# A remade instruction order for a gated spectral/MLP mix: packed inverse rows, paired inverse tables, all weight splits remade on chip

## Chip, cores and metric

One core of one Trainium2 chip. The metric is the device time of one execution in microseconds (us), the median of several runs of each kernel.

## The reference, cut to what matters

```python
def reference(A_x, A_w_r, A_w_i, B_x, B_w1, B_b1, B_w2, B_b2, gate_w):
    x = A_x                                             # (1, 2048, 512), fp32
    g = sigmoid((x * gate_w).sum(-1, keepdims=True))
    a = irfft2(rfft2(x) * (w_r + 1j * w_i))             # over (2048, 512)
    b = gelu(x @ w1 + b1) @ w2 + b2                     # 512 -> 1792 -> 512
    return g * a + (1 - g) * b
```

## The kernel before, in words

**Products.** TensorE (PE) multiplies in the float32r format. A full fp32 operand is therefore kept as two tiles, a rounded high part `h` and the rest `l`, and a product is three matmuls (hh, hl, lh). Further matmuls are saved by a seven-product scheme (Strassen's) on pairs of the 14 blocks of 128 hidden columns (`seven`, L1093 on): its sums and differences of weights are made for the first half of the tokens (tiles `wA..`), stored in DRAM as `su` by L1085, and loaded again for the second half as `wB0h`, `wBth`, `wBsl` and so on (`raw`, issued through L411).

**Stages.** The 2048 rows are 16 tiles `j` of 128. `forward(j)` (L571) folds a tile and multiplies it by the tables of the column transform (`pd`) and of the row transform (`py`, tables `tf`), which gives `y`, one tile [128, 2, 257] per j. `stage1` (L745) is a radix-4 pass over the `y` tiles. Then come four passes of the MLP for the first half of the tokens, `group("A", p)` (L1138), with the filter `filt(q0)` (L749), which multiplies each `y` by a loaded tile `wf` (load L757; a small ACT operation on it L758, products `m` on DVE, L761). `stage4` (L783) is the last radix pass; the row 64 of its tiles is turned separately in `ownx`/`ownz` (load L796, store L802). `inverse(c, h)` (L804) handles two tiles at a time: it loads the tables `tg` (L810) and multiplies them by the gate `gb` (L811), loads the rows of `y` with halves exchanged into `sw` (L823, two loads of 63 rows for a tile; the two rows left are cleared by a memset on POOL, L819), forms `pq` (L825), multiplies (`pz`), splits the result into `zb` (L837 and L838), multiplies by `ci` (`pa`) and combines (`od`, `u`, `v`). `group("B", p)` is the MLP for the second half of the tokens, with the inverse transform of the other half running among it; `last` (L987) writes the output.

**Down projection.** `down` (L945) adds the blocks of a pass into a PSUM bank `po`. From the second pass on, the sum so far, `s`, is first copied into the bank by ACT (L966), and after the pass `po` is copied back to `s`. The weights are `wb0` to `wb13`, each as `h` and `l`. `load_w` (L886) makes them with `halve` (L878): one load of the raw weights into what will be `l` (L880), an ACT copy to `h` (rounding), an ACT copy of `-h` into `l` (L475), and a DMA on POOL's queue that adds the raw weights onto it from DRAM (L408, an accumulating DMA). The first half of the tokens (A) and the second (B) each need all 14 blocks. For blocks f below `KEPT` (10) the B passes make them again in this way; for f = 10 to 13, L904 stores `h` and `l` in DRAM (`sb..`) and the last B pass loads them (`wb10hb`, `wb10lb` and so on).

**What sets the order.** Every step is put into a graph (L228 to L345) with an engine, a cost and a lag. None of that is scheduled at run time: a long list, `ORDER`, gives the order in which steps are emitted, and each engine (PE, DVE, ACT, POOL and SP, which issues nearly all plain DMAs) works through its own steps in that order, waiting at each for what it needs. A second list, `SLOTS`, gives each tile its place among a few of its kind (7 of `t2k`, 3 tables `ttab`, 8 of `xhl`, 46 work tiles `w` of 256 KB, 8 PSUM banks); a tile's first writer waits for the last reader of the tile that had the place before. The costs in `dma`, `store` and `acc` (L400 to L408) belong to the search that made the lists and change nothing by themselves.

Of the kernel before, what the change touches and what calls it, by code (L numbers as in the profile page):

```python
# [10 lines left out]
F32 = mybir.dt.float32  # L11
F32R = mybir.dt.float32r
AF = mybir.ActivationFunctionType
ALU = mybir.AluOpType
# [12 lines left out]
KEPT = 10  # L27
# [28 lines left out]
def _tables():  # L56
# [39 lines left out]

    turn = np.pi * np.arange(NJ).reshape(4, 4) / NJ
# [251 lines left out]
def tile_kernel(ctx: ExitStack, tc: tile.TileContext, xt, xc, w1, w2, b1, b2, x0g, wf, wrev, out, consts):  # L349
# [50 lines left out]
    def dma(emit, kb, reads, writes, lag=3.4):  # L400
        return add("sp", 0.62 if kb == 257 else 0.47, lag, emit, reads, writes, kb / 340)

    def store(emit, kb, reads, writes):
        return dma(emit, kb, reads, writes, 3.8)
# [858 lines left out]
```

## Time and profile before

| | |
|---|---|
| median of 3 runs | 363.33 us (361.85 to 365.05) |
| the profiled execution | 362.7 us, its span 360.9 us |
| granted TensorE clock | 0.997 |
| DMA | 76.67 MB, mean 212 GB/s |
| plain DMA queue (q1) | 65.70 MB, 57.0% of 16 engines' span |
| software (accumulating) queue (q0) | 10.27 MB, 18.6% |

The profile's engines are PE (matmul), PEld (weight load, overlapping PE), DVE, ACT, POOL; SP issues DMAs, and SPq, DVEq and the like are the engines' queues, where issuing and waiting stand. A line "A Lx t <- B Ly: 3.1, 1, 3.1" in the table of waits says that engine A at line x, tile t, waited 3.1 us in all, once, longest 3.1 us, for what engine B did at line y (for a DMA, the transfer's names). The chain is followed back from the last instruction, through what released each; its rows are start, length, what. All matmuls go through one helper, so they have the line L414 and are told apart by tile. The idle time in 20 us stretches comes from the table of stretches, which gives for each the busy time of every engine.

### The profile page before, as it was taken

The numbers are of one execution on the slowest core, as the hardware profiler recorded it, in microseconds if no ns is written. First come the engines' busy times: TensorE is split into PE (matmuls) and PEld (weight loads), VectorE is DVE, ScalarE is ACT, GpSimd is POOL, SyncE is SP. The second block draws the span as 40 slices with busy tenths as digits, with TensorE's granted clock in tenths as the row PEclk, the third lists the DMA queues.
The fourth block names the chain that finished last, engine by engine and source line by source line (L and its number), as shares of the span: only waits on it lengthen the run. The fifth ranks groups of instructions, "written<-read, shape, count | busy, mean of one in ns | idle before, by whom it ended". The sixth has DMA issues, their size and how long they took to land.

```text
span 360.9 us, 5784 instructions
## 1 busy us (share of the span) xinstructions
PE 349.3 (97%) x1760; PEld 294.0 (81%) x1760; DVE 324.3 (90%) x681; ACT 266.7 (74%) x572; POOL 54.6 (15%) x84
## 2 busy tenths in 40 slices
PE   7999999999999999989999999999999999999994
PEld 6988888888887888868887888888888877788884
DVE  4999997989899999799999999999999787799951
ACT  4999999999999679767587993578866364577521
POOL 1012002001013002200010110002341330003320
PEclk9999999999999999999999999999999999999998
DMA  7999989249787947979996665696781678625697
GB/s 221 380 289 260 342 282 239 91 136 251 205 199 176 319 169 194 266 276 291 291 301 192 119 178 121 204 271 186 169 211 60 182 220 235 187 79 107 123 236 240
DMA packets 52041, 76.67 MB, mean 212 GB/s; under 512 B 5833, under 2 KB 23689, under 8 KB 52009
## 3 DMA queue, kind: packets, MB, share of 16 engines
q1 hardware_dynamic: 44728, 65.70, 57.0%
q0 software_dynamic: 6848, 10.27, 18.6%
q10 hardware_dynamic: 432, 0.33, 0.3%
q8 instruction: 14, 0.23, 0.3%
q14 instruction: 19, 0.15, 0.1%
HBM read 52.54 MB, written 19.41 MB: 199 GB/s over the span
## 4 chain that ended last, share of the span: by engine, by line
PE 82%; DMA 8%; SPq 5%; DVE 2%; issue 1%; ACT 1%; POOL 0%; DVEq 0%; POOLq 0%
PE po L414 39%; PE uxA L414 8%; PE uxB L414 8%; PE nuA L414 6%; PE nuB L414 6%; PE pd L414 4%; PE py L414 3%; PE ph L414 3%; SPq L823 2%; DMA wf<-in_wf 2%; PE pz L414 2%; DMA wBth<-su 2%; PE pa L414 2%; DMA g<-in_x0g 1%; DMA sw<-y 1%
## 5 line engine op out<-in xcount | busy, mean ns | idle before, releaser
L966 ACT ACTIVATE po<-s 128x512 f32<-128x512 f32 (+1 forms) x49 | 28.9, 595 | 10.1 <-DVE t L1004 4.7
L423 ACT ACTIVATE s<-po 128x512 f32<-128x512 f32 x40 | 23.5, 596 | 4.8 <-PE po L414 4.3
L761 DVE TENSOR_TENSOR m<-y,wf 128x514 f32<-128x514 f32 x32 | 21.4, 689 | 0.5
L819 POOL MEMSET sw<- 1x512 f32 x32 | 16.6, 518 | 27.9 <-PE po L414 15.2
L414 PE MATMUL py<-zb,tf 128*128 128x258 f32 x96 | 20.7, 297 | 0.0
L414 PE MATMUL pz<-tg,pq 128*128 128x128 f32 x128 | 18.9, 276 | 1.5 <-DVE tg L811 1.3
L414 PEld LDWEIGHTS pz<-tg,pq 128*128 128x128 f32 x128 | 17.4, 190 | 3.5 <-issue 1.8
L414 PE MATMUL pd<-cf,w 128*128 128x129 f32 x128 | 18.5, 275 | 0.3 <-DVE cf L533 0.3
L414 PEld LDWEIGHTS pd<-cf,w 128*128 128x128 f32 x128 | 17.2, 190 | 1.5 <-DVE cf L533 0.5
L976 ACT ACTIVATE s<-po,b2t 128x512 f32<-128x512 f32 x16 | 10.9, 690 | 9.6 <-PE po L414 9.6
L414 PE MATMUL pa<-zb,ci 128*128 128x256 f32 x96 | 17.3, 289 | 0.6 <-DVE zb L838 0.6
L414 PEld LDWEIGHTS py<-zb,tf 128*128 128x128 f32 x96 | 15.8, 189 | 2.1 <-ACT logit L617 0.2
L414 PEld LDWEIGHTS pa<-zb,ci 128*128 128x128 f32 x96 | 15.1, 189 | 2.9 <-DVE zb L838 1.0
L414 PE MATMUL nuB<-xB,wB0h 128*128 128x512 f32 x56 | 17.4, 391 | 0.0
L825 DVE TENSOR_TENSOR pq<-y,sw 128x256 f32<-128x256 f32 x32 | 12.8, 417 | 4.2 <-DMA sw<-y 3.3
L618 DVE TENSOR_TENSOR zb<-pd,zb 128x256 fp32r<-128x256 f32 x32 | 13.2, 419 | 3.6 <-ACT logit L617 3.5
L408 POOL DMA_DIRECT2D w<-bacc x8 | 9.6, 1255 | 41.3 <-ACT fiveB L423 26.7
L414 PE MATMUL nuA<-xA,wA0h 128*128 128x512 f32 x48 | 15.1, 396 | 0.0
L837 ACT ACTIVATE zb<-pz 128x512 fp32r<-128x512 f32 x16 | 9.0, 595 | 7.1 <-PE pa L414 4.8
L638 ACT ACTIVATE y<-pys 64x257 f32<-64x257 f32 x32 | 13.3, 417 | 0.9 <-DVE pys L635 0.3
L423 ACT ACTIVATE od<-pa 128x512 f32<-128x512 f32 x8 | 4.8, 598 | 11.9 <-PE pa L414 8.7
L408 POOL DMA_DIRECT2D wA0l<-in_w x6 | 5.4, 956 | 52.2 <-DMA tf<-tf 22.1
(541 smaller groups left out, 1240.8 us busy)
## 6 DMA issues: line engine op xcount, KB each, us to landing
wf<-in_wf SPq DMA_DIRECT2D x16, 257.0 KB
sw<-y SPq DMA_DIRECT2D x32, 126.0 KB
xf<-in_xt SPq DMA_DIRECT2D x14, 256.0 KB
tf<-tf SPq DMA_DIRECT2D x16, 192.0 KB
wrA<-in_w SPq DMA_DIRECT2D x12, 256.0 KB
xbA<-in_xc SPq DMA_DIRECT2D x8, 256.0 KB
xbB<-in_xc SPq DMA_DIRECT2D x8, 256.0 KB
bacc<-s SPq DMA_DIRECT2D x8, 256.0 KB
```

The costliest lines, as they stand in the source:

```text
L408: return add("pool", 0.9, 3.8, lambda: nc.gpsimd.dma_start(dst(), src(), accum_op=ALU.add), reads, writes, 2.3 * kb / 340)
L414: pe.matmul(ps, w, x, start=start, stop=stop, **more)
L423: a(lambda: act.activation(o.ap(), i.ap(), AF.Copy, scale=scale), n, [i], [o])
L618: v(lambda c=c: vec.tensor_tensor(segs(xl, c), both(c), segs(xh, c), op=ALU.subtract), 256, [ps[c], (xh, c)], [(xl, c)])
L638: a(lambda o=o, i=i: act.activation(Y[j].ap()[o:o + HP, 1], pys.ap()[i:i + HP, 1], AF.Copy), 257, [(pys, 1)], [(Y[j], 1 + k)], more=0.07)
L761: v(lambda mk=mk, k=k, y=y, w=w: vec.tensor_tensor(mk.ap(), y.ap(), w.ap()[:, k:k + 1, :ND].to_broadcast([P, 2, ND]), op=ALU.mult), 514, [ ...
L819: nc.gpsimd.memset(sw.ap()[o:o + 1], 0.0)
L823: dma(lambda sw=sw, y=y, o=o, i=i: sp.dma_start(sw.ap()[o + 1:o + HP], y.ap()[i + 1:i + HP, :, :HD]), 160, [y], [(sw, k)], 3.4)
L825: v(lambda sw=sw, pq_=pq_, y=y, k=k, op=op: vec.tensor_tensor(pq_.ap()[:, k], y.ap()[:, k, :HD], sw.ap()[:, 1 - k], op=op), 256, [y, TURNE ...
L837: a(lambda n=n, ps=ps: act.activation(zh.ap()[:, :, :, n], ps.ap(), AF.Copy), 512, [ps], [(zh, n)])
L966: a(lambda ps=ps, n=n, o=o: act.activation(ps.ap(), o.ap()[:, n], AF.Copy), size, [o], [ps], more=0.04)
L976: a(lambda o=o, ps=ps, q=q: act.activation(o.ap(), ps.ap(), AF.Identity, bias=b2t.ap()[:, q:q + 1]), 600, [b2t, ps], [o])
```

## The change

1. `ORDER` and `SLOTS` are made anew, 2105 steps for 2121, after the search's costs were set to other values (plain DMA lag 3.4 to 3.1 and rate 340 to 350, store lag 3.8 to 3.2, accumulating DMA lag 3.8 to 3.3).
2. `KEPT` goes from 10 to 14: no split is kept in DRAM. The eight stores of `sb10` to `sb13` and the eight loads in the last B pass go; in their place that pass makes four blocks by `halve`: four loads of raw weights, eight ACT operations, four accumulating DMAs. (The `if` of L904 and the `else` in `group` are still there, without use.)
3. The tables `tg` are laid out in pairs: each `inverse(c, h)` loads one tile of 128 KB and multiplies it once over 256 columns, in place of two loads of 64 KB and two multiplies of 128.
4. `stage4` writes its outputs packed (`YP`: the two halves of 256 follow each other, 2 KB of one piece a row, in place of two pieces of 1 KB in rows of 257), `ownx`, `ownz` and `sw` use them so. The `sw` loads move the same bytes.

Some steps and where they stand in the two lists (entry of 2121, entry of 2105):

| step | before | after |
|---|---|---|
| load of `wf6`, whose ACT step waits in the profile | 1026 | 1167 |
| load of `wBth3` | 1234 | 1152 |
| `tg`: first and last table load | 1395, 1990 | 1473, 1916 |

The diff without the two lists:

```diff
-KEPT = 10
+KEPT = 14
...
     ti[:, HP] = 1.0 - 2.0 * (np.arange(P) % 2)
+    ti = ti.reshape(2, 2, 4, P, P).transpose(2, 0, 3, 1, 4).reshape(4, 2, P, 2 * P)
...
-    def dma(emit, kb, reads, writes, lag=3.4):
-        return add("sp", 0.62 if kb == 257 else 0.47, lag, emit, reads, writes, kb / 340)
+    def dma(emit, kb, reads, writes, lag=3.1):
+        return add("sp", 0.62 if kb == 257 else 0.47, lag, emit, reads, writes, kb / 350)
     def store(emit, kb, reads, writes):
-        return dma(emit, kb, reads, writes, 3.8)
+        return dma(emit, kb, reads, writes, 3.2)
     def acc(dst, src, kb, reads, writes):
-        return add("pool", 0.9, 3.8, lambda: nc.gpsimd.dma_start(dst(), src(), accum_op=ALU.add), reads, writes, 2.3 * kb / 340)
+        return add("pool", 0.92, 3.3, lambda: nc.gpsimd.dma_start(dst(), src(), accum_op=ALU.add), reads, writes, 2.2 * kb / 350)
...
+    def packed(t):
+        return t.rearrange("p a b -> p (a b)")[:, :D].rearrange("p (a b) -> p a b", a=2)
+
+    YP = [View(yy, 3 * j, 3, lambda t, j=j: packed(t[:, j])) for j in range(NJ)]
...
     def stage4(j0):
         ys = [Y[j0 + 4 * q0] for q0 in range(4)]
-        radix4(ys, [j0 * q0 for q0 in range(4)], 1, HD, ys, f"d{j0}")
-        x, z = (t2k(f"own{n}{j0}", cls="own", parts=2) for n in "xz")
+        radix4(ys, [j0 * q0 for q0 in range(4)], 1, HD, [YP[j0 + 4 * q0] for q0 in range(4)], f"d{j0}")
+        x, z = (t2k(f"own{n}{j0}", HD, cls="own", parts=2) for n in "xz")
...
         def rows():
-            return yy.ap()[HP:HP + 1, j0::4].rearrange("p j a b -> p j (a b)")
+            return yy.ap()[HP:HP + 1, j0::4].rearrange("p j a b -> p j (a b)")[:, :, :D]
...
     def inverse(c, h):
+        tg = buf("ttab", [P, 2 * P], F32, f"tg{c}{h}", cls="tg")
+        dma(lambda: sp.dma_start(tg.ap(), ti_d[c, h]), 128, [], [tg])
+        v(lambda: vec.tensor_tensor(tg.ap(), tg.ap(), gb.ap()[:, c, 2 * h * P:(2 * h + 2) * P], op=ALU.mult), 2 * P, [gb], [tg])
         for n, j in enumerate((c + 8 * h, c + 8 * h + 4)):
-            t = buf("ttab", [P, P], F32, f"tg{j}", cls="tg")
-            dma(lambda t=t, j=j: sp.dma_start(t.ap(), ti_d[j]), 64, [], [t])
-            v(lambda t=t, j=j: vec.tensor_tensor(t.ap(), t.ap(), gb.ap()[:, j % 4, j // 4 * P:(j // 4 + 1) * P], op=ALU.mult), P,
-              [gb], [t])
-            y = Y[j]
+            y = YP[j]
...
-                dma(lambda sw=sw, y=y, o=o, i=i: sp.dma_start(sw.ap()[o + 1:o + HP], y.ap()[i + 1:i + HP, :, :HD]), 160, [y], [(sw, k)], 3.4)
+                dma(lambda sw=sw, y=y, o=o, i=i: sp.dma_start(sw.ap()[o + 1:o + HP], y.ap()[i + 1:i + HP]), 130, [y], [(sw, k)], 4.0)
...
-                    mm(ps.ap()[:, ft, k], pq_.ap()[:, k, ft * P:(ft + 1) * P], t.ap(), True, True)
+                    mm(ps.ap()[:, ft, k], pq_.ap()[:, k, ft * P:(ft + 1) * P], tg.ap()[:, n * P:(n + 1) * P], True, True)
```

More of the change, by code (lines that the diff above doesn't have):

```diff
@@ L793, in rows @@
         def rows():
-            return yy.ap()[HP:HP + 1, j0::4].rearrange("p j a b -> p j (a b)")
+            return yy.ap()[HP:HP + 1, j0::4].rearrange("p j a b -> p j (a b)")[:, :, :D]
         dma(lambda: sp.dma_start(flat(x.ap()[:4]), rows()), 8, ys, [x], 4.5)
-        a(lambda: act.activation(z.ap()[:4, :, :HD], x.ap()[:4, :, :HD], AF.Copy, scale=al.ap()[:, j0, 1:2]), 512, [x, al], [z], more=0.1)
+        a(lambda: act.activation(z.ap()[:4], x.ap()[:4], AF.Copy, scale=al.ap()[:, j0, 1:2]), 512, [x, al], [z], more=0.1)
         for k, op in enumerate((ALU.subtract, ALU.add)):
             v(lambda k=k, op=op: vec.scalar_tensor_tensor(
-                x.ap()[:4, k, :HD], x.ap()[:4, k, :HD], al.ap()[:, j0, 0:1], z.ap()[:4, 1 - k, :HD], op0=ALU.mult, op1=op), 256,
+                x.ap()[:4, k], x.ap()[:4, k], al.ap()[:, j0, 0:1], z.ap()[:4, 1 - k], op0=ALU.mult, op1=op), 256,
                 [z, al], [(x, k)], more=0.055)
@@ L822, in inverse, with turn @@
             for k, (o, i) in enumerate(((0, HP), (HP, 0))):
-                dma(lambda sw=sw, y=y, o=o, i=i: sp.dma_start(sw.ap()[o + 1:o + HP], y.ap()[i + 1:i + HP, :, :HD]), 160, [y], [(sw, k)], 3.4)
+                dma(lambda sw=sw, y=y, o=o, i=i: sp.dma_start(sw.ap()[o + 1:o + HP], y.ap()[i + 1:i + HP]), 130, [y], [(sw, k)], 4.0)
             for k, op in enumerate((ALU.subtract, ALU.add)):
                 v(lambda sw=sw, pq_=pq_, y=y, k=k, op=op: vec.tensor_tensor(
-                    pq_.ap()[:, k], y.ap()[:, k, :HD], sw.ap()[:, 1 - k], op=op), 256,
+                    pq_.ap()[:, k], y.ap()[:, k], sw.ap()[:, 1 - k], op=op), 256,
                     [y, TURNED[c], sw], [(pq_, k)])
             ps = bank([P, 2, 2, P], f"pz{j}", "pz")
-            def turn(k, t=t, ps=ps, pq_=pq_):
+            def turn(k, n=n, ps=ps, pq_=pq_):
                 for ft in range(2):
-                    mm(ps.ap()[:, ft, k], pq_.ap()[:, k, ft * P:(ft + 1) * P], t.ap(), True, True)
+                    mm(ps.ap()[:, ft, k], pq_.ap()[:, k, ft * P:(ft + 1) * P], tg.ap()[:, n * P:(n + 1) * P], True, True)
             for k in range(2):
-                add("pe", c_pe4(P, 2), 0.25, lambda k=k, turn=turn: turn(k), [t, (pq_, k)], [ps])
+                add("pe", c_pe4(P, 2), 0.25, lambda k=k, turn=turn: turn(k), [tg, (pq_, k)], [ps])
             a(lambda n=n, ps=ps: act.activation(zh.ap()[:, :, :, n], ps.ap(), AF.Copy), 512, [ps], [(zh, n)])
```

200 rows, old and new, of tables (ORDER, SLOTS) are left out of this document.

## The prediction

> **What bounds the kernel now.** I read the page first, for the engine that ends last.
>
> ```profile
> PE 349.3 (97%) x1760; PEld 294.0 (81%) x1760; DVE 324.3 (90%) x681; ACT 266.7 (74%) x572; POOL 54.6 (15%) x84
> ...
> PE 82%; DMA 8%; SPq 5%; DVE 2%; issue 1%; ACT 1%; POOL 0%; DVEq 0%; POOLq 0%
> ```
>
> TensorE (PE) is busy 349.3 of 360.9 us, and the change leaves its 1760 matmuls alone. So only its idle time can move: 11.6 us. The 18% of the chain that is not PE names what PE waits for: transfers (8%) and SP's issuing queue (5%). The table of stretches tells where the idle time is.
>
> ```profile
> 0.00:20.00 20.00, 17.84 (x109) 15.56 (x110) 15.41 (x48) 14.14 (x46) 2.29 (x13) 1.00 0.91 308
> 140.00:160.00 20.00, 18.39 (x80) 14.61 (x79) 16.92 (x34) 14.46 (x31) 2.60 (x3) 1.00 1.00 295
> 180.00:200.00 20.00, 19.16 (x85) 15.58 (x85) 19.83 (x39) 16.23 (x33) 3.52 (x5) 1.00 0.79 232
> 280.00:300.00 20.00, 19.21 (x113) 16.60 (x112) 16.33 (x38) 9.48 (x18) 7.24 (x14) 1.00 0.74 207
> 300.00:320.00 20.00, 18.64 (x105) 15.44 (x104) 15.54 (x38) 10.54 (x20) 0.00 (x0) 1.00 0.63 186
> 340.00:361.00 21.00, 16.04 (x85) 13.60 (x83) 9.29 (x17) 5.14 (x12) 4.42 (x4) 0.95 0.91 221
> ```
>
> After the length come busy PE, PEld, DVE, ACT and POOL, the granted clock, the DMA share and GB/s. The clock is 1.00, so nothing is throttled. PE's idle time is 2.16 at the start, 1.61, 0.84, 0.79 and 1.36 in the four middle stretches (4.60 together), 4.96 at the end; every other stretch is full. Next the waits, first of all engines and then PE's own, and the chain in order of time.
>
> ```profile
> DVE tg L811 <- DMA tg<-ti: 3.7, 3, 1.6
> DVE pq L825 <- DMA sw<-y: 3.3, 2, 2.2
> ACT wf L758 <- DMA wf<-in_wf: 3.1, 1, 3.1
> ```
>
> ```profile
> PE po L414 <- ACT po L966: 1.4, 1, 1.4
> PE pz L414 <- DVE tg L811: 1.3, 2, 0.8
> PE uxB L414 <- DMA wBth<-su: 0.8, 1, 0.8
> PE pa L414 <- DVE zb L838: 0.6, 1, 0.6
> ```
>
> ```profile
> 127.48 1.36 PE uxA L414 x6
> ...
> 147.09 8.77 DMA wf<-in_wf
> ...
> 184.13 6.75 DMA wBth<-su
> 191.03 1.61 PE uxB L414 x6
> ...
> 289.57 3.73 DMA tg<-ti
> ...
> 305.45 4.02 DMA sw<-y
> ...
> 343.57 12.48 PE po L414 x66
> ```
>
> Three separate stories. (A) At 147.09 a `wf` load is issued while the DMA engines are full (share 1.00); it lands 8.77 us later. ACT stands 3.1 us at L758, and the bias copy `po` (L966) behind it on ACT makes PE wait. (B) At 184.13 the load of `wBth` lands 6.75 us later, 0.8 us too late. (C) From 282 to 315 PE waits for the inverse's tables `tg` and swapped rows `sw`.
>
> "Busy" ends are modelled, so a pause is partly booked as work. I therefore also set each matmul's start against the work ahead of it at the undisturbed pace (1.36 for six of 512 columns, the first line above). By that account A costs 2.1, B 1.0 and C 4.0 us: 7.1 in the middle, against the floor of 4.6 from the table. I use 7.1, and the floor for the range. A slow drift of 1.5 us between 20 and 105 us stays as it is.
>
> **Change, part by part. The order.** I walked both lists and gave each step its place in TensorE work. For A, the raw load of `wb10l` moves up from 128 to 101 us of work and its ACT pieces from 143 to 128, so less is issued beside the `wf` load; every `wf` load now has over 9.5 us from the release of its slot to its use, above the 8.77 it took in a full stretch. For B, the load has 17.7 us ahead of its user instead of 6.1, against 6.75 measured; the shortest such loop up to 190 is 8.8. I take both as gone: 2.1 + 1.0 = 3.1, bounds 2.4 (1.61 + 0.84) and 3.1. If that cover fails again, each costs what it costs now.
>
> **Fewer splits in DRAM.** Eight stores of 256 KB leave the time around A and B, eight loads become four, and four accumulating loads on POOL and eight ACT operations are added, all for the last pass.
>
> ```profile
> L475 ACT ACTIVATE wb13l<-wb13h x1: 616/616/616, 143.3 to 143.3; 128x512 fp32r<-128x512 f32 x1
> L408 POOL DMA_DIRECT2D wb13l<-in_w x1: 1320/1320/1320, 145.0 to 145.0; - x1
> ...
> DMA to landing us min/median/max: 9.4/9.4/9.4
> ```
>
> Those 2 MB are 7 us of DMA time at the 295 GB/s of the full stretch; that supports taking them as gone, and isn't counted twice. ACT gets 8 x 0.62 = 5.0 us more between about 260 and 330, where it is busy 9.48 and 10.54 of 20: hidden, 0 (5.0 if all of it stood ahead of a bias copy). Four accumulations at 0.85 to 1.32 are 3.4 to 5.3 us of POOL, idle from 300 to 320: 0. They landed after up to 9.4 us when queued together; the new order leaves 11.4 us between `wb10l`'s ACT copy and its first matmul. So 0, with 2.0 us to spare; each further us of lateness of ACT there would cost a us.
>
> **Tables in one transfer.**
>
> ```profile
> L811 DVE TENSOR_TENSOR tg<-tg,gb x16: 274/285/293, 249.1 to 329.5; 128x128 f32<-128x128 f32 x16
> ```
>
> ```profile
> L810 SPq DMA_DIRECT2D tg<-ti x16: 318/373/1483, 221.4 to 323.5; - x16
> ```
>
> ```profile
> L825 DVE TENSOR_TENSOR pq<-y,sw 128x256 f32<-128x256 f32 x32 | 12.8, 417 | 4.2 <-DMA sw<-y 3.3
> ```
>
> Eight SP issues fewer, 8 x 0.37 = 3.0 us over 100 us. DVE does eight multiplies of 256 columns (0.417, as `pq`) for sixteen of 0.285: 3.3 for 4.6, 1.2 us less, off PE's path. What counts is earliness: in the old list nine tables have 5.7 to 7.0 us of PE work from the release of their slot to their use, against 3.73 of landing and the queue on SP ahead of it; in the new one half are loaded 20 to 60 us ahead, and the short ones have 6.6, 8.0, 8.0 and 8.7.
>
> **One-piece rows.** SP issues without a pause from 278 to 310.
>
> ```profile
> 284.63 0.81 SPq L823
> 285.44 0.06 issue
> 285.56 0.80 SPq L823
> ```
>
> ```profile
> L823 SPq DMA_DIRECT2D sw<-y x32: 787/808/1097, 244.8 to 308.5; - x32
> ```
>
> ```profile
> L757 SPq DMA_DIRECT2D wf<-in_wf x16: 540/551/1207, 97.7 to 210.4; - x16
> ```
>
> ```profile
> L796 SPq DMA_DIRECT2D ownx<-y x4: 661/662/687, 247.3 to 291.1; - x4
> ```
>
> No row shows a packed swap's issue, so it is built up: a table of 128 one-piece rows takes 0.37; `wf`, 128 rows of two pieces, 0.55, so the second piece costs 0.18; `ownx`, four one-piece rows, 0.66, so a count of rows other than 128 costs 0.29. Together 0.84, and the swap (63 rows, two pieces) shows 0.81: the parts add up. Without the second piece the swap is 0.81 - 0.18 = 0.63, say 0.65; bounds 0.37 (as the tables) and 0.81 (nothing gained; a loss is excluded, since pieces get fewer and bytes don't change). The new order puts 23 swaps among the issues of that busy stretch: 23 x 0.16 = 3.7 us of SP less. With SP's own issue time laid into the loops, the old list's loops that stalled had 4.4 to 5.5 us left for landing. The new list has at least 5.0 with 0.65, at least 6.2 with 0.45, but 3.2 to 4.5 in four loops with 0.81. So at 0.65 C goes from 4.0 to about 1.25: the smallest loops stand at the edge of what stalled. Gain 2.75, bounds 0 and 4.0.
>
> [...]
>
> **Start.**
>
> ```profile
> 6.39 1.58 PE L414 MATMUL ph<-xf,war 128*128 128x128 f32 x12 [0.80 <-DMA war<-in_w]
> 8.26 1.83 PE L414 MATMUL pd<-cf,w 128*128 128x129 f32 x14 [0.30 <-DVE cf L533]
> ```
>
> ```profile
> 10.43 0.89 PE ph L414 x8
> ```
>
> By the code three pieces of the fp32 product `ph` are done before the first `pd`: 4, 4 and 8 records, at 0.89 for eight 1.78 us (four of the sixteen are missing in the row). The new list keeps the first ahead and puts the other two, 1.33 us, behind; the `cf` copy moves ahead of one `w` multiply (0.36), so `pd` starts that much earlier. At worst 1.33 - 0.36 = 0.97 is lost; PE's pauses from 8.26 to 20, 0.54 by the account of starts, can take up the rest, so 0.43 at best. I take 0.5. After 20 us DVE and ACT are as far ahead of PE as before, within 1 us. **End**: the last 12.48 us of `po` and the stores behind are the same in both lists: 0.
>
> **Sum**, against the profiled execution (362.7 us, span 360.9, 1.8 around it): -3.1 (A, B) - 2.75 (C) + 0.5 (start) = -5.35, thus 357.35. The median of the runs lies 0.63 higher, at 363.33: **358.0 us**.
>
> **Rivals.**
> 1. *Swaps stay at 0.81 us, or tables and swaps are late again.* For it: no row shows a packed swap, and four loops of the new list are then shorter than those that stalled. Against: the parts added up. C stays at 4.0 to 5.0: -3.1 + 0.5 + 0 to 1.0, about 361.2. [...]
> 2. *All pauses go.* For it: half of C's tables are far ahead. Against: SP still serves some 30 us without much slack. -7.1 + 0.5: 356.7; with the drift gone as well, 355.2.
> 3. *Slower: a load listed early blocks SP.* SP issues in order; a load whose slot isn't free holds all behind it. The new list puts half of the tables (L810) 20 to 60 us ahead, among the `wf` and `wB` loads.
>
> ```profile
> SPq L757 <- DVE m L761: 29.2, 8, 12.8
> SPq L810 <- PE pz L414: 12.8, 5, 4.4
> ```
>
> It has held 12.8 us. The shortest loops up to 190 us have 8.8 us, 2.05 more than the 6.75 of landing; a hold of 12.8 ahead of one makes it 10.75 late: -5.35 + 10.75 = +5.4, 368.7. It costs from 2.05 us of hold beyond what the list has counted, and turns the sign from 2.05 + 5.35 = 7.4. Against: I counted the loops from the slot's release, so it bites only where DVE, which frees the slots, runs behind the list; and the longest holds of before cost PE nothing.
> 4. *It does not do what it says*: the list is new, but lateness moves to other loads (the new costs count shorter latencies, 3.1 for 3.4 us, than the 3.73 to 8.77 shown above), and 5 us come back elsewhere: 363.
>
> **Chances.** Forecast 0.50 (357.0 to 359.6 by itself), rival 1 0.20, rival 2 0.15, rival 3 0.09, rival 4 0.06. A measurement of this kernel tells about 1% (3.6 us) from no change. Below 359.7 lie the forecast and rival 2: 0.65. Within 1% lie rivals 1 and 4 and the smallest holds of rival 3: 0.27. Above 367.0: 0.08. The range goes from 355.0 (rival 2 with the drift) to 362.5 (rival 1 with the floor on A and B, 2.4, the worst start, 0.97, and half a us more in C: 0.9 of gain, 362.4).
>
> **What would show it.** Swaps' issue near 0.65 us on SP; no wait of ACT for `wf` and of `uxB` for `wBth`; PE over 19.7 in 140 to 160 and 180 to 200, and idle below 1 us in 280 to 320; the first `pd` near 7.9 and 0.5 us less done by 20 us; no wait of `po` for POOL's `wb10l`. I'd be wrong in the size if swaps still took 0.8, and in the sign if SP stood over 7 us at one load while PE waited for another behind it.

## The result and the profile after

The changed kernel takes 366.31 us (median of 16 runs, 364.62 to 367.97) against 363.09 for the one before (16 runs, 360.93 to 365.05): ratio 1.0082, 95% interval 1.0062 to 1.0102. The forecast was 358.0, range 355.0 to 362.5: the time lies outside it and went the other way. It lies within the 1% that was called no change, to which 0.27 was given; 16 runs on each side tell the 0.8% from none.

The profiled execution took 366.0 us, its span 363.9 (before 362.7 and 360.9). The stretches that held PE's idle time before, and the two that hold it now (length, busy PE, PEld, DVE, ACT, POOL, granted clock, DMA share, GB/s):

```profile
0.00:20.00 20.00, 17.48 (x116) 15.73 (x117) 15.88 (x50) 15.04 (x49) 3.14 (x14) 1.00 0.90 303
...
140.00:160.00 20.00, 20.00 (x89) 16.54 (x89) 19.86 (x41) 16.97 (x34) 3.45 (x4) 1.00 0.99 294
...
180.00:200.00 20.00, 20.00 (x90) 16.57 (x89) 19.77 (x42) 18.25 (x35) 1.81 (x3) 1.00 0.69 208
...
260.00:280.00 20.00, 16.75 (x81) 13.29 (x79) 16.32 (x33) 10.95 (x19) 4.15 (x8) 1.00 0.46 137
280.00:300.00 20.00, 17.61 (x91) 15.65 (x92) 15.85 (x33) 7.29 (x13) 5.18 (x10) 0.85 0.67 183
300.00:320.00 20.00, 20.00 (x121) 17.70 (x121) 17.64 (x40) 13.08 (x24) 0.38 (x1) 0.98 0.50 148
```

A and B are gone: PE is full from 20 to 260 us. In exchange 260 to 300, where it lost 0.8 us, now has 5.6 us of idle time, and the granted clock falls to 0.85. The waits name two new things (all engines first, then PE's own):

```profile
DVE y L677 <- DMA y<-ownx: 6.1, 2, 3.1
...
DVE pq L829 <- DMA sw<-y: 3.6, 1, 3.6
```

```profile
PE pz L416 <- DVE pq L829: 2.1, 1, 2.1
PE pz L416 <- DVE tg L816: 2.0, 1, 2.0
PE po L416 <- DVE g_3l L472: 1.5, 1, 1.5
```

The same account of starts as in the prediction (start of each matmul less the work ahead of it at the undisturbed pace; us lost by that time) sets the two side by side:

| by | 20 | 140 | 200 | 260 | 280 | 300 | 320 | end |
|---|---|---|---|---|---|---|---|---|
| before | 7.0 | 8.5 | 11.8 | 11.8 | 11.9 | 13.2 | 15.8 | 16.2 |
| after | 7.0 | 8.3 | 8.3 | 8.3 | 10.4 | 17.8 | 18.6 | 19.0 |

At 260 us the changed kernel is 3.5 us ahead. In the next 60 it loses 10.3 us, the one before 4.0. The difference at the end, 2.8, is the span's 3.0 within 0.2.

The first new wait is a surprise of the packing. `radix4` writes its second and fourth outputs with one instruction over two tiles at once (`mixed`). On the packed rows two of these writes in `stage4` wait in the trace for a transfer of own rows of *another* set of tiles (3.0 us at 257, 3.1 at 275); with the rows unpacked (e2 below) none does. Nothing in the data calls for it: by the code the tiles written and the rows moved are different ones. The chain in order of time shows one, and the second new thing behind it:

```profile
275.22 3.33 DMA y<-ownx
278.55 0.03 issue
278.58 0.02 DVEq L677
278.60 0.05 issue
278.65 1.29 DVE y L677 x2
279.94 0.34 DVE tg L816
280.29 0.04 issue
280.33 1.16 PE pz L416 x4
281.49 0.85 PE pa L416 x4
282.35 2.83 PE po L416 x9
```

DVE, in order, stands 3.1 us before `y`; the table multiply `tg` queued behind is late, and PE with it. Then PE itself is slow: 9 matmuls of `po` take 2.83 us, where the pace before was 1.36 for six. Single rows of PE's timeline, start, length:

```profile
277.90 0.40 PE L416 MATMUL po<-g_2h,wb2l 128*128 128x512 f32 x1
280.33 1.16 PE L416 MATMUL pz<-tg,pq 128*128 128x128 f32 x4 [2.04 <-DVE tg L816]
281.14 1.20 PE L416 MATMUL pa<-zb,ci 128*128 128x256 f32 x4
282.14 0.63 PE L416 MATMUL po<-g_3h,wb3h 128*128 128x512 f32 x1
282.57 0.63 PE L416 MATMUL po<-g_3l,wb3h 128*128 128x512 f32 x1
283.00 0.63 PE L416 MATMUL po<-g_3h,wb3l 128*128 128x512 f32 x1
283.42 0.59 PE L416 MATMUL po<-g_3h,wb3h 128*128 128x512 f32 x1
283.85 0.40 PE L416 MATMUL po<-g_3l,wb3h 128*128 128x512 f32 x1
284.09 0.40 PE L416 MATMUL po<-g_3h,wb3l 128*128 128x512 f32 x1
```

From 282.14 on the starts are 0.43 us apart, from 283.85 on 0.24: after a pause of 2.04 us PE ran at half speed for 3.5 us (granted clock 0.52 from 280.30 to 283.85). The pause at 262 (1.55 us) had no such tail, the one at 296 (2.1) had one again. By the account of starts the three pauses cost 2.1, 3.9 and 4.1 us, of which the slow clock is 1.7 and 1.6. That is this one execution; of the 16 runs, the one with a granted clock of 1.000 over its whole span took 366.59 us, so the median does not rest on the slow clock. The length of the pause alone does not decide: in e1 below, pauses of 2.4 and 2.0 us were not followed by a slow clock.

The second new thing: from 265.5 to 272.9 SP stands 7.3 us at one swap (L827, tile 1, used after 300 us) for rows that DVE has not written, then issues nearly back to back to 302; the swaps' issue time did fall, to 0.71. DVE was not late against the kernel before: there it wrote these rows at 275.6 us or later, here at 272.2. Their swap stands earlier in the new list, ahead of others whose rows were ready.

```profile
SPq L827 <- DVE y L677: 7.3, 1, 7.3
```

```profile
272.15 0.69 DVE L677 SCALAR_TENSOR_TENSOR y<-d1s,d1s 128x512 f32<-128x512 f32 x1
```

```profile
L827 SPq DMA_DIRECT2D sw<-y x32: 697/708/858, 247.6 to 308.4; - x32
```

### The profile page after: what moved, and what is told of

Read it like the earlier page. It is cut to its first block, busy times and chain, and to the rows that moved or that the text cites. A ratio compares the mean times of both kernels' runs of the same rounds, so it can differ in the third digit from the quotient of the medians.

```text
span 363.9 us, 5766 instructions
## 1 busy us (share of the span) xinstructions
PE 350.7 (96%) x1760; PEld 297.0 (82%) x1760; DVE 324.7 (89%) x673; ACT 271.4 (75%) x580; POOL 57.9 (16%) x88
## 4 chain that ended last, share of the span: by engine, by line
PE 85%; DVE 7%; DMA 4%; issue 1%; SPq 1%; ACTq 0%; ACT 0%; DVEq 0%
PE po L416 37%; PE uxA L416 9%; PE uxB L416 8%; PE nuA L416 7%; PE nuB L416 6%; PE pd L416 4%; PE pz L416 4%; PE py L416 3%; PE ph L416 3%; PE pa L416 3%; DMA sw<-y 2%; DVE y L677 1%; DMA bacc<-s 1%; DMA y<-ownx 1%; DMA xf<-in_x0g 1%
## 5 line engine op out<-in xcount | busy, mean ns | idle before, releaser
L416 PE MATMUL pz<-tg,pq 128*128 128x128 f32 x128 | 20.1, 289 | 4.1 <-DVE pq L829 2.1
L416 PEld LDWEIGHTS pz<-tg,pq 128*128 128x128 f32 x128 | 18.4, 201 | 5.6 <-DVE tg L816 2.5
L416 PE MATMUL pa<-zb,ci 128*128 128x256 f32 x96 | 18.3, 303 | 0.0
L416 PEld LDWEIGHTS py<-zb,tf 128*128 128x128 f32 x96 | 16.2, 189 | 2.2
L829 DVE TENSOR_TENSOR pq<-y,sw 128x256 f32<-128x256 f32 x32 | 12.8, 419 | 3.7 <-DMA sw<-y 3.6
L645 ACT ACTIVATE y<-pys 64x257 f32<-64x257 f32 x32 | 13.2, 417 | 1.6 <-DVE pys L642 1.0
L911 ACT ACTIVATE uxB<-uxB,b1t 128x512 f32<-128x512 f32 x14 | 9.2, 665 | 6.1 <-DVE uxB L1117 5.5
L586 DVE TENSOR_TENSOR eo<-xf 128x256 f32<-128x256 f32 x32 | 12.7, 419 | 0.5 <-DMA xf<-in_x0g 0.3
L589 DVE TENSOR_TENSOR w<-eo 128x256 f32<-128x256 f32 x32 | 12.9, 419 | 0.2
```

Source lines behind the costliest of these rows:

```text
L416: pe.matmul(ps, w, x, start=start, stop=stop, **more)
L586: v(lambda s=s, op=op: vec.tensor_tensor(eo.ap()[:, s], x.ap()[:, 0:2], x.ap()[:, 2:4], op=op), 256, [x], [(eo, s)])
L589: v(lambda s=s, op=op: vec.tensor_tensor(w.ap()[:, s], eo.ap()[:, :, 0], eo.ap()[:, :, 1], op=op), 256, [eo], [(w, s)])
L645: a(lambda o=o, i=i: act.activation(Y[j].ap()[o:o + HP, 1], pys.ap()[i:i + HP, 1], AF.Copy), 257, [(pys, 1)], [(Y[j], 1 + k)], more=0.07)
L829: v(lambda sw=sw, pq_=pq_, y=y, k=k, op=op: vec.tensor_tensor(pq_.ap()[:, k], y.ap()[:, k], sw.ap()[:, 1 - k], op=op), 256, [y, TURNED[c], ...
L911: a(lambda: act.activation(ps.ap(), ps.ap(), AF.Gelu_apprx_tanh, bias=b1t.ap()[:, f:f + 1]), 600, [b1t], [ps]).table = "gelu"
```

## The experiments

Theory 1 began as: the packed rows' extra waits on DVE are the cause. Theory 2: SP's queue between 278 and 302 is, by the new list or the number and length of its issues. In e5 and e7 the names stand for two halves of the second: the list's order on SP (1), or the issues' number and length (2). Ratios are to the kernel before, measured beside each.

**The two-tile write split (e1), the rows unpacked (e2), the old kernel with packed rows (e3), filler work in the pauses (e4).**

```diff
# e1: radix4, for stage 4 only
-        fma(mixed(0), turned(D1), -h, w(D0), 2 * n, [D0, D1], [outs[1], outs[3]])
+        halves((part(outs[1], 0), part(outs[3], 1)), (part(D1, 1), part(D1, 0)), -h, (part(D0, 0), part(D0, 1)), n, ...)
...
# e2 (and the other way round e3, on the kernel before)
-            y = YP[j]
+            y = Y[j]
...
# e4: in turn()
+                if k == 0 and j in (10, 7):
+                    for _ in range(8):
+                        mm(ps.ap()..., CI[0].ap()[:, 0, 0, 0], CI[0].ap()[:, 0]..., True, True)
```

e1. 

> The changed kernel, with stage 4's write into two tiles at once (radix4's mixed) made as two instructions of one tile each, so that DVE no longer waits there for the own-row transfers of another set of tiles. DVE does sixteen 256-wide operations (0.42 us) for eight of 0.69, 1.2 us more. Theory 1 (those waits are the cause: DVE stood 3.0 and 3.1 us at 257 and 275, PE paused three times and lost 2.1, 3.9 and about 4.1 us with the slow clock after two of them): the first two pauses go, 6 us, and the third goes or shrinks since the swaps' loads behind DVE's late rows come earlier: 356 to 360.5, granted clock 1.00 in 280 to 300. Theory 2 (the new list has SP too late by itself; DVE's standing only fills time that PE loses anyway): 364 or more, with pauses of PE at about the same places.

Measured: 363.79 us, 1.0037 (1.0005 to 1.0070). In the profile DVE's two stands are gone and so are PE's first two pauses (10.4 lost by 260, 11.1 by 280); but 280 to 300 now loses 5.1, and PE waits for transfers:

```profile
PE nuB L416 <- DMA wB0l<-su: 2.4, 1, 2.4
PE pz L416 <- DVE pq L844: 2.0, 1, 2.0
```

```profile
280.00:300.00 20.00, 15.56 (x90) 13.22 (x89) 14.20 (x32) 7.94 (x14) 5.18 (x10) 1.00 0.67 199
```

Between the two expectations: some 1.6 us of the ratio came back, not 6 to 10. The first half of theory 1 holds, the third pause did not go with the others. In the profiles 260 to 320 loses 7.1 us for 10.3, and that difference, 3.2, is no more than the slow clock (3.3), which is missing here although PE paused for 2.4 and 2.0 us. What the first two pauses had cost came back as waits for what SP issues.

e2. 

> The changed kernel with the rows of stage 4 unpacked again, as before (pieces of 1 KB, own rows whole, swaps of two pieces); order, tables in pairs and splits as changed. The write into two tiles waits for no transfer here. Theory 1: the pauses after DVE's standing go, but swaps take 0.81 us of SP for 0.71, 2.3 us more over the 23 of the busy stretch: 357 to 362, slower than the split write by 0 to 2. Theory 2: SP is later still, 366 to 369.

Measured: 364.33 us, 1.0048 (1.0013 to 1.0082), with the same two pauses of PE (`wB0l` 2.7, `pz` 1.9); after the first of them the clock did fall here (0.83 in 280 to 300). So DVE's waits for own rows belong to the packing, and the 0.1 us of each packed issue can't be told from nothing in this pair.

e3. 

> The kernel before with only the packed rows: old order, tables and splits. Here the write of the set j0=1 waits for the own-row store of j0=3 (issued at 272.5, the write came at 274.9), and that of j0=0 for a load issued at 278.3. Theory 1: DVE stands 1 to 2 us at about 275 and the swaps take 0.71 us of SP: 362 to 365, the wait on DVE is shown. Theory 2 (packing is harmless, and the list alone is at fault): no wait on DVE for own rows, 360 to 363.

Measured: 362.61 us, 1.0018 (0.9988 to 1.0048). In the old list the own rows had landed in time: DVE stood at none of them, which theory 1 had wrong for this kernel. Packing alone, with the swaps at 0.75 us, buys nothing measurable.

e4. 

> The changed kernel with eight filler matmuls of 512 columns (1.8 us, overwritten afterwards, no part of the result) in PE's queue ahead of the two pz at which it paused for 2.2 and 2.3 us; all waits stay. If the slow clock after these pauses (matmul of 512 columns 0.43 for 0.23 us, granted clock 0.85 in 280 to 300) comes from PE standing idle, the clock stays at 1.00 and 2.5 to 3.3 us come back: 363 to 364. If it comes from something else in this stretch: 366 to 367.

Measured: 365.52 us, 1.0092 (1.0051 to 1.0133). The clock stayed full in the profiled run, with the pauses filled (over all runs its mean is 0.997, in the changed kernel 0.992):

```profile
280.00:300.00 20.00, 17.94 (x102) 14.80 (x101) 15.20 (x32) 7.46 (x14) 5.17 (x10) 1.00 0.59 176
```

```profile
PE nuB L416 <- DMA wB0l<-su: 1.7, 1, 1.7
```

That fits PE's standing idle as what slows the clock (0.85 in this stretch of the changed kernel, 1.00 here); but e1 kept 1.00 with pauses of 2.4 and 2.0 us, so such a pause was not always followed by the fall. The time won came back as a new wait: PE was ready for a transfer at 291.4 us, 1.0 earlier than in the changed kernel, and the transfer, issued at 288.5 for 287.3, was there at 293.1. This is a sign that something in front of PE sets the pace up to 302 us.

**The order on SP (e5, e6), half of the swaps on ACT (e7), half of them with 64 rows (e8).**

```diff
# e5 (on e1) and e6 (on the changed kernel)
+    late = [1605, 1614, 1613, 1639, 1649, 1798]   # swaps of tiles 1, 5, 5, 9, 13, 12
+    numbers = [n for n in numbers if n not in late]
+    at = numbers.index(1949) + 1                  # the load of wBsl5
+    numbers[at:at] = late
...
# e7 (on e1)
-                ... sp.dma_start(sw.ap()[o + 1:o + HP], y.ap()[i + 1:i + HP])
+                ... (act if k else sp).dma_start(sw.ap()[o + 1:o + HP], y.ap()[i + 1:i + HP])
...
# e8 (on e1)
+                    if k:
+                        sp.dma_start(sw.ap()[HP:], y.ap()[:HP])
+                        nc.gpsimd.memset(sw.ap()[HP:HP + 1], 0.0)
```

e5. 

> The split write, and six entries of the order moved: the swap loads of tiles 1, 5, 9, 12 and 13, which are used after 300 us, now stand behind the load of wBsl5 instead of 5 to 20 SP issues earlier. In the split write SP stood 8.3 us at the first of them (for the rows of set j0=1) with eleven loads behind it, then issued without a pause from 278 to 302, and PE paused 2.7 us for wB0l and 2.3 us for a swap of tile 7. Theory 1 (the list's order on SP: late-needed swaps ahead of early-needed loads): both pauses go, 357 to 360. Theory 2 (SP has simply too many and too long issues there): the sum of issues is the same, the pauses move but stay, 362.5 to 364.5.

Measured: 362.65 us, 0.9995 (0.9967 to 1.0024), the time that the second expectation had. But it decides nothing: the stand at the swap is down to 1.8 us, and SP now stands 6.8 us at the next load in the list, for PE. 260 to 320 loses 7.0 us where e1 lost 7.1, and the pauses named gave way to another:

```profile
SPq L899 <- PE po L416: 6.8, 1, 6.8
```

```profile
PE pz L416 <- DVE zb L857: 2.6, 1, 2.6
```

e6. 

> The same six entries moved, with the write into two tiles left whole as in the changed kernel, so that DVE still waits for the own-row transfers of another set. If those waits cost by themselves (3.0 us at 257, 3.1 at 275, PE 2.1 and 2.2 us and the slow clock behind the second): 361 to 363.5, two pauses of PE left at 262 and 280. If they only mattered through SP: as the split write with the entries moved, 357 to 360.

Measured: 366.65 us, 1.0102 (1.0056 to 1.0148). DVE stands 4.5 us at `y` and 4.0 at `pq` for own rows:

```profile
DVE y L677 <- DMA y<-ownx: 4.5, 2, 3.1
DVE pq L829 <- DMA y<-ownx: 4.0, 1, 4.0
```

With the same order the whole write costs 1.0102 - 0.9995 = 0.0107, 3.9 us. So the extra waits cost by themselves. The changed kernel against e1 gives 0.0045, 1.6 us; by the intervals of the runs these are 3.9 within 2.0 and 1.6 within 1.4, so that the one is larger is not shown.

e7. 

> The split write, order as changed, with one of the two swap loads of each tile issued from ACT's queue instead of SP's: 16 x 0.71 = 11.4 us of issuing leave SP, ACT (busy 8 to 13 of 20 us there) gets as much. Theory 2 (the number and length of SP's issues): the pauses of 2.7 and 2.3 us go, 357 to 360. Theory 1: the swap that holds SP for 8.3 us is one of the moved ones, so this takes away the hold too: also 357 to 360, unless ACT in its place stands at it and its copies come late: 363 to 367.

Measured: 374.23 us, 1.0297 (1.0231 to 1.0363): worse than either theory had it. PE waited 4.7 us for ACT's copies into `po` and 4.3 for `pz`, and ACT stood 4.7 us ahead of `g_5h` for nothing that the profile names, which fits the swaps holding ACT as they held SP. It tells nothing for or against SP's length.

e8. 

> The split write, with the swap load that reads rows 0 to 63 taking all 64 rows instead of 63 (row 64 of the swap tile is then cleared by the same memset, now after the load). [...]

Measured: 362.01 us, 0.9955 (0.9926 to 0.9983).

```profile
L843 SPq DMA_DIRECT2D sw<-y x16: 478/534/1146, 247.9 to 302.6; - x16
```

```profile
L846 SPq DMA_DIRECT2D sw<-y x16: 697/768/851, 249.6 to 297.9; - x16
```

64 rows take 0.53 us of SP, 63 rows 0.77 in the same kernel: 0.23 less for one row more. 0.53 is above the 0.39 of a table of 128 rows in the changed kernel (L815), so one row more doesn't take away all that a swap's issue costs above a table's. All 32 swaps take 21.4 us of SP, e1's 23.5, and 260 to 320 loses 4.4 us instead of e1's 7.1.

**All together (e9, e10), more issues (e11), the start alone (e12).**

```diff
# e10: e1 + e8 + the moved entries of e5; e9: also, and e12 on the changed kernel alone
+    for n, ahead in ((489, 13), (496, 37), (497, 37)):
+        numbers.remove(n)
+        numbers.insert(numbers.index(ahead), n)
...
# e11 (on e1), behind eight swaps
+                        sp.dma_start(more[:, m], w1[m][:, :4])
```

e9. 

> All changes together: the split write, half of the swaps with 64 rows, the swaps of tiles 1, 5, 9, 12 and 13 moved behind wBsl5, and at the start the three fp32 pieces of ph ahead of the first pd again, as before (with the second half of war loaded before the tables cf). Theory: each part takes away one of the causes (DVE's standing, SP's queue, the slow clock and the 1.3 us of moved work at the start): 357 to 360, granted clock 1.00 up to 280, PE's idle time in 280 to 320 below 3 us. [...]

Measured: 360.11 us, 0.9939 (0.9899 to 0.9979), 0.1 above the 357 to 360 expected.

e10. 

> As the run before without the start's part. If the start matters (three of seven profiles of the new start had a granted clock of 0.72 from 6 to 12 us and 2.0 us more lost by 20 us): slower than that run by 0.6 to 2 us. If the slow clock there comes at random to any start: the same within 0.5 us.

Measured: 359.37 us, 0.9923 (0.9888 to 0.9957): faster than both kernels. 260 to 320 loses 3.5 us, most of it in one stretch:

```profile
280.00:300.00 20.00, 18.06 (x113) 15.84 (x112) 16.62 (x39) 10.01 (x18) 8.56 (x17) 1.00 0.76 218
```

Its intervals overlap e9's: the start makes no difference that these runs can tell.

e11. 

> The split write with eight more DMA issues on SP (8 KB loads of no use, 0.35 to 0.4 us each, 3 us in all) right behind eight of the swaps between 280 and 290. If SP's queue sets the pace of that stretch, PE's pauses at 292 and 296 grow by about as much: 366 to 368 against 363.8 for the split write. If the pauses come from the landing of single transfers or from DVE: 363.5 to 364.5.

Measured: 366.34 us, 1.0113 (1.0076 to 1.0150), 0.0076 or 2.8 us over e1. The eight issues (16 bytes in each of 128 rows, 2 KB and not the 8 of the expectation) took 0.47 us each, with the gap behind each 0.5, so about 4 us; by the account of starts 280 to 300 loses 8.9 us, 3.8 more than in e1, and the waits of PE grew at the same two places:

```profile
PE nuB L416 <- DMA wB0l<-su: 3.7, 1, 3.7
PE pz L416 <- DVE pq L853: 2.8, 1, 2.8
```

```profile
280.00:300.00 20.00, 13.53 (x73) 11.56 (x72) 12.40 (x29) 6.42 (x12) 4.86 (x10) 0.83 0.54 165
```

The two waits grew by 2.1 us together, about half of the issue time added; most of the rest of the 3.8 is the clock, which fell here (0.83) and not in e1. In the median the 4 us cost 2.8. So time added to SP's queue reaches PE: the queue sets the pace of this stretch. It does not yet say why the queue is late.

e12. 

> The changed kernel with the start alone as before (three pieces of ph ahead of the first pd). By PE's pace 1.33 us of work comes back into the time before the first pd, which starts some 0.4 later: 0.5 to 1 us faster where the clock was full, 2 to 2.5 where it was slow: median 364 to 365.5 against 366.3, granted clock 1.00 from 6 to 12 us. If the work ahead made no difference: 366 to 367.

Measured: 366.57 us, 1.0114 (1.0032 to 1.0197): nothing gained that four runs can tell. Nothing here says that the time went at the start.

**SP's idle time filled (e13), with 64 rows (e14), with the whole write (e15).** Five swaps of tiles 3, 7 and 11 have their rows and places by 262 us, and so have one table and one store; the list puts them behind the swap at which SP stands.

```diff
# e13 (on e1), e14 (on e8), e15 (on the changed kernel)
+    early = [1349, 1379, 1380, 1357, 1358, 1376, 1006]
+    numbers = [n for n in numbers if n not in early]
+    at = numbers.index(1605)                      # the swap of tile 1
+    numbers[at:at] = early
```

e13. 

> The split write (e1), with seven entries of the order moved ahead of the swap at which SP stood 8.3 us: five swaps of tiles 3, 7 and 11, whose rows and places are free by then, one table and one store, 4.6 us of issuing that the list has among the crowd of 278 to 302. The number of issues is the same. If SP's idle time ahead of the crowd is the cause: the pauses of 2.4 (wB0l) and 2.0 us (pz) go, 260 to 320 loses 3 us or less instead of 7.1, 358.5 to 360.5. If the number and length of issues decide whatever their order: 362.5 to 364.5.

Measured: 357.71 us, 0.9859 (0.9829 to 0.9889). The same 289 issues, and the pauses are gone:

```profile
260.00:280.00 20.00, 20.00 (x103) 16.92 (x103) 18.50 (x41) 12.01 (x21) 4.73 (x10) 1.00 0.62 198
280.00:300.00 20.00, 19.98 (x123) 17.63 (x122) 19.23 (x45) 11.72 (x21) 4.58 (x9) 1.00 0.70 211
300.00:320.00 20.00, 20.00 (x121) 17.48 (x120) 18.55 (x41) 15.09 (x29) 3.42 (x4) 1.00 0.47 103
```

SP's own rows (start, time of the issues, count) show what fills the time in which it stood:

```profile
264.00 0.47 SPq L413 DMA_DIRECT2D wB0h<-su  x1
264.52 3.71 SPq L842 DMA_DIRECT2D sw<-y  x5
268.34 0.41 SPq L830 DMA_DIRECT2D tg<-ti  x1
268.80 0.42 SPq L1001 DMA_DIRECT2D bacc<-s  x1
271.80 0.76 SPq L842 DMA_DIRECT2D sw<-y  x1
```

SP stands 2.5 us at the swap instead of 8.3. 260 to 320 loses 1.4 us (8.6 to 10.1). The order on SP was the cause; the number and length of its issues, the same here as in e1, are not.

e14. 

> As e13 with 64 rows for half of the swaps (e8). If SP's queue is what is left to cost: 357 to 359.5, 260 to 320 loses 2.5 us or less. If e13 already has SP out of the way: the same as e13 within 0.7.

Measured: 357.24 us, 0.9866 (0.9820 to 0.9913): as e13. With SP out of the way the cheaper issues of e8 are worth nothing that shows.

e15. 

> The same seven entries moved in the changed kernel itself, with the write into two tiles left whole. DVE still waits for own rows of another set: 3 to 4 us behind e13, as e6 was behind e5, 362 to 364.5. If those waits cost only where SP is late too: as e13.

Measured: 360.77 us, 0.9954 (0.9925 to 0.9983), 0.0095 or 3.4 us behind e13, from which it differs in the code only by the whole write, which brings DVE's extra waits (5.7 us) back:

```profile
DVE y L677 <- DMA y<-ownx: 5.7, 2, 3.6
```

## Why the prediction was wrong, by its own steps

**A and B (-3.1): right, in mechanism and size.** By the account of starts 2.2 and 1.1 us are gone, with nothing in their place up to 260. No wait for `wf` or `wBth` is left.

**Splits in DRAM (0): right.** `wb10l` landed after at most 4.9 us, and PE waited for none of the remade weights.

**Start (+0.5): 0.0 in the profile (7.0 us lost by 20 us in both).** Four of thirteen profiles with this start (e1, e5, e6, e15) lose about 2 us more there, with a granted clock of 0.72 between 6 and 12 us; the four profiles with the old start (the kernel before, e3, e9, e12) show 1.00. Whether the new start favours the slow clock stays open: four profiles are too few, and the times of e9 and e12 show no gain.

**One-piece rows (-2.75 in stretch C): the step that failed.** Its price was near: 0.71 us of issue where 0.65 was taken (the second piece was worth 0.10, not 0.18). The tables did as forecast: DVE's 3.7 us of waits for their loads are gone. But its sentence "the new list has at least 5.0" us in the loops was wrong, for two reasons, and C went from 4.0 us to 10.3.

- The loops ran from the release of a slot, with SP free to issue from then on. SP takes its list in order, and a swap also waits for the rows that it reads. The new list puts the swap of tile 1 where DVE has not yet written them; SP stood 7.3 us, and the five swaps behind it, which had been issued by 274 us in the list before, came into the crowd of 278 to 302 (18 swaps there for 14). Given to SP in its idle time, they bring back 5.7 us of C (e1 to e13), and 6.5 us or so of the median.
- Packing was counted as an edit of transfers. It also changed which instructions wait for which, and DVE got waits that no term of the sum had: 1.6 us (e1), 3.9 (e6 against e5), 3.4 (e15 against e13), within 1.4 to 2.0 each, so the runs do not tell these three apart.

The slow clock after a pause, 3.3 us of C in the profiled execution, was in no term either; there it makes two pauses of two us cost nearly four each. What it costs the median stays open: e4, with a clock nearer to full, was no faster that the runs can tell (1.0092 for 1.0082).

**The sum was of terms that are not independent.** A and B bring PE 3.5 us earlier to a stretch that SP paces; in e4 PE arrived there 1.0 us earlier and then waited 1.7 us for `wB0l`, so that the runs tell no time won. With both errors, of the list and of the write, out of the way (e13) the kernel takes 357.71 us, within 0.3 of the forecast, and C loses 1.4 us where 1.25 was forecast. That agreement is in part luck: e13 runs another list than the one forecast, and its gain in C comes from the order on SP, while the prediction took it from the cheaper issue of packed rows, which has no part in it that shows (e2 against e1, e3, e14).

**The rivals.** The third, "a load listed early blocks SP", was the mechanism, and 0.09 was too little for it. It had the tables waiting for their slots in mind; it was a swap, waiting for DVE. Its terms were near: it turned the sign from a hold of 7.4 us, and SP stood 7.3 with DVE's extra waits beside it; the prediction's own sign for an error of direction, SP over 7 us at one load with PE waiting for another behind it, came true. The evidence was in the prediction's own list of SP rows, where one hold of 12.8 us was called free because PE had not paid for it before, and in a row of the same table that it does not show: the swaps of the kernel before already stood for rows that DVE had not written.

```profile
SPq L823 <- DVE y L670: 7.1, 3, 4.4
```

## What to carry to other kernels

In this kernel SP's queue passed its wait of 7.3 us at one swap on to the five swaps behind it: for each entry of such a queue that can wait, list what stands behind it that is ready, and when that is needed. Price an edit of a layout by the waits in the generated program as well as by the transfers; here the instruction that writes two tiles at once got waits of 3.0 and 3.1 us that its data do not call for. Before adding up gains along the bound engine, ask what paces the stretch in which the time won would be spent.

## What the runs showed of the hardware that was not expected

- A pause of 2.04 us on PE was followed by 3.5 us at half speed (a matmul of 512 columns every 0.43 us for 0.23); a pause of 1.55 was not, and neither were pauses of 2.4 and 2.0 in e1. With the pauses filled by matmuls of no use the clock stayed at 1.00 in the profiled run (e4).
- A DMA of 64 rows took 0.53 us of SP's time, one of 63 rows of the same width 0.77, and a load of 128 rows of 16 bytes 0.47.
